# Block means in one bank and three pieces, held stores of x, and a smaller transfer scratch, in an attention and expert kernel on one core

## The chip, the core and the metric

One core of a Trainium2 chip runs one program. Its engines are TensorE (PE), VectorE (DVE), ScalarE (ACT), GpSimd (POOL) and SyncE (SP); they run side by side, each works through its own list in order, and semaphores hold them to one another. PE writes to PSUM banks; DVE and ACT read them. SP and POOL issue the transfers between HBM and SBUF, which share 16 DMA engines. The metric is the device time of one launch in microseconds (us), lower is better.

## The reference

Attention with a local window and block summaries, for 4 batches, 8 heads, 768 positions and 64 channels, then a layer of 8 experts in which each token goes to one expert of bounded size.

```python
k_sum = k.reshape(B, H, nb, block, D).max(axis=3)       # block = 32, nb = 24
v_sum = v.reshape(B, H, nb, block, D).mean(axis=3)
scores_l = scale * q @ k^T, kept where |i - j| < 16
scores_s = scale * q @ k_sum^T + log(block)
a = softmax(concat(scores_l, scores_s))                 # sum + 1e-09
attn = a @ concat(v, v_sum)                             # -> x, 3072 x 512
logits = x @ w_gate                                     # 8 experts
# the largest logits first: each token to one expert, at most 384 tokens each
out[mask_e] = relu(x[mask_e] @ w1[e]) @ w2[e]
```

## The kernel before

**Two parts.** The attention part takes the 24 tiles of 128 query rows in order (t = 0 to 23, six tiles a batch, each tile two units u of 64 rows), writes x to HBM (`xd`) and keeps the logits. The routing picks 384 tokens for each expert in turn; each expert gathers its rows of x, multiplies twice and scatters its result. Only the attention part is touched by the change, with one parameter of the whole program.

**One tile.** PE makes the scores s(t) (four pairs of heads, L365), DVE adds the mask and takes the minimum (m, L373), ACT takes the exponential (e, L380), PE transposes (t, L141), ACT or DVE copies the transposed weights out of PSUM (c, `pt`), PE multiplies them with the window of v (pv, L401), DVE divides by the sum, which is a column of ones beside v (n, L430 to L433, written into `XS[t]`, four buffers in turn), POOL stores the tile (xw, L494), PE transposes x (xt, L141), ACT copies it (xf), and for four tiles at a time PE makes the logits (lg, L472) with a copy, a transpose and a copy behind them (ly, lt, lc).

**One batch.** SP loads keys (`kd`, four loads p = 0 to 3 of 0.41 MB), queries (`qt`) and twelve windows of v (`vw`, 0.2 MB each, task w). From batch 1 on each load waits until an earlier one has landed, so that some 1.3 MB are in flight. DVE takes the maxima of the keys' blocks (`ks`, L289); POOL copies the windows of keys and the maxima into `kw` (two L202 copies for each p; batch 0 has them on ACT and DVE). The block means of v go into the first 24 rows of each of the twelve windows of v: PE multiplies the windows of v with a small matrix (vm, L305, 12 matmuls for each half g of the heads), a copy takes the result out (vmc, `vm`), PE adds the pieces (vb, L332), a copy writes the sums into the first window (vbc, `vw`), and POOL copies them into the other eleven (place, L341).

**PSUM.** Bank x (one buffer) holds the x transposes, and from batch 1 on also each vm and vb. Bank l holds the logits. For batch 0 vm takes x and l, and vb two banks of the output.

**Order.** No order is written down. Every step is a task with an engine (or two to choose from), a cost in us, the tasks that it needs, and a rank; `plan` runs a small model and each time emits the task that can start first, by rank. `TUNE` holds the offsets of the ranks. The order so found is what each engine then follows on the chip, whatever the real times are.

```python
if b:
    @task(("vm", b, g), "pe", 1.6, [("w", u0 + i) for i in range(NQ)] + ["constants"]
          + ([("vbc", b, 0)] if g else [("xf", u0 // 2 - 4)]), u0 - TUNE["vm"] + 0.1 * g)
```

So from batch 1 on, each half of the means needs all twelve windows of v, and the second half also needs the first half's result.

Of the kernel before, what the change touches and what calls it, by code (L numbers as in the profile page):

```python
# [8 lines left out]
F32 = mybir.dt.float32  # L9
# [47 lines left out]
def attention_moe(ctx, tc, qT, kT, v65, wg, w1r, w2r, cst, out, dbg=None, dbi=None):  # L57
# [148 lines left out]
    with ExitStack() as att:  # L206
# [16 lines left out]
        XR = 6  # L223

# [17 lines left out]
        for i in range(2):  # L242
            nc.gpsimd.memset(VW[i][:NB], 0.0)
# [6 lines left out]
        @task("constants2", "sp", 1.4, [], -10, 0.9)  # L250
        def _():
            nc.sync.dma_start(cs[:, CA:], cst[:, CA:CW])
            XS[0] = sb.tile([128, H * D], F32, name="x", bufs=4)
            nc.sync.dma_start(XS[0][:, :TW], cst[:, CW:])
            nc.sync.dma_start(wgs[:, :, :E], wg)
# [16 lines left out]
        for b in range(B):  # L272
# [30 lines left out]
            def means(b, g, k):  # L303
                for j in range(4):
                    nc.tensor.matmul(VP[b, g][32 * j:32 * j + 32], own[:C, k], VW[b % 2][:C, 4 * k + j, 4 * g:4 * g + 4].rearrange("k h d -> k (h d)"), start=k == 0, stop=k == 2)  # L305

            for k in range(3 if b == 0 else 0):
                @task(("vm", 0, k), "pe", 1.0, [("w", 4 * k + i) for i in range(4)] + ["constants"], -TUNE["vm"] + 0.1 * k)
                def _(k=k):
                    for g in range(2):  # L310
                        if k == 0:
                            VP[0, g] = psum.tile([128, 512], F32, name="xl"[g])[:, :4 * VD]
                        means(0, g, k)

            for g in range(2):
                if b:
                    @task(("vm", b, g), "pe", 1.6, [("w", u0 + i) for i in range(NQ)] + ["constants"]
                          + ([("vbc", b, 0)] if g else [("xf", u0 // 2 - 4)]), u0 - TUNE["vm"] + 0.1 * g)
                    def _(b=b, g=g):
                        VP[b, g] = psum.tile([128, 512], F32, name="x")[:, :4 * VD]  # L320
                        for k in range(3):
                            means(b, g, k)

                @task(("vmc", b, g), {"act": 0.42, "dve": 0.4}, None, [("vm", b, g if b else 2)], u0 - TUNE["vm"])
                def _(eng, b=b, g=g):
                    VM[b, g] = sb.tile([128, 4 * VD], F32, name="vm", bufs=2)
                    copy(eng, VM[b, g], VP[b, g])

                @task(("vb", b, g), "pe", 0.45, [("vmc", b, g)], u0 - TUNE["vm"])
                def _(b=b, g=g):  # L330
                    VB[b, g] = psum.tile([128, 512], F32, name="x" if b else f"o{g}")[:NB, :4 * VD]
                    nc.tensor.matmul(VB[b, g], blocks, VM[b, g], start=True, stop=True)  # L332

                @task(("vbc", b, g), {"act": 0.42, "dve": 0.4}, None, [("vb", b, g)] + ([("pv", u0 - 2 * NQ + 1)] if b > 1 else []), u0 - TUNE["vm"])
                def _(eng, b=b, g=g):
                    copy(eng, VW[b % 2][:NB, 0, 4 * g:4 * g + 4].rearrange("k h d -> k (h d)"), VB[b, g])

            for i in range(1, NQ):
                @task(("place", b, i), "pool", 0.58, [("vbc", b, 1)] + ([("pv", (u0 + i - 2 * NQ) | 1)] if b > 1 else []), u0 - TUNE["vm"] + 0.1 * i)
                def _(b=b, i=i):  # L340
                    nc.gpsimd.tensor_copy(VW[b % 2][:NB, i], VW[b % 2][:NB, 0])  # L341
# [4 lines left out]
        for u in range(U):  # L346
# [42 lines left out]
            def _(eng, u=u):  # L389
# [4 lines left out]
                  [("c", u), ("c", u | 1 if t < NT - 1 else u), ("w", u | 1), ("w", u & ~1)] + ([("place", b, (i - s) + x) for x in range(2) if i - s + x] + [("vbc", b, 1)])  # L394
# [14 lines left out]
        def used(t):  # L409
            return ("lg" if t < FOURS else "l", last_of(t))  # L410

        for t in range(NT):
            u = 2 * t + 1
            spare = t >= NT - 2
            for k, half in enumerate(halves(t)):
# [6 lines left out]
                      + ([("xw", t - 4), ("xt", t - 4)] if t >= 4 else []), u + TUNE["n"])  # L422
                def _(t=t, half=half):
                    if half.start == 0:
                        XS[t] = sb.tile([128, H * D], F32, name="x", bufs=4)
# [6 lines left out]
                    for g in gs:  # L432
# [4 lines left out]
                      [("n", t) + me] + [("vbc", b, 1) for b in range(B) if t == max(0, b * NQ // 2 - 3)] + ([("xf", t - 1)] if t and not spare else [("c", U - 1)] if t == NT - 1 else [("xf", t - 1)] if t else []), u + TUNE["xt"])  # L437
# [25 lines left out]
                if t < FOURS:  # L463
                    if t == last_of(t):
                        t0 = t - QUAD + 1

                        @task(("lg", t), "pe", 0.9, [("xf", j) for j in range(t0, t + 1)] + ["constants2"] + ([("lc", t0 - 1)] if t0 else []), u + TUNE["l"])
# [6 lines left out]
                        @task(("ly", t), "act", 0.25, [("lg", t)], u + TUNE["l"] + 0.1)  # L474
                        def _(t=t):
                            LY[t] = sb.tile([128, 128], F32, name="ly")
                            nc.scalar.activation(LY[t], PL[t][:, :128], AF.Copy)
# [14 lines left out]
            @task(("xw", t), "pool", 0.6, [("n", t)], u, 0.73)  # L492
            def _(t=t):
                nc.gpsimd.dma_start(xd[t * 128:(t + 1) * 128], XS[t])  # L494
# [488 lines left out]
```

## Time and profile before

| | us |
|---|---|
| median of 3 runs | 474.02 (473.02 to 474.35) |
| the profiled execution, its own time | 473.94 |
| its span, first to last instruction | 472.2 |
| attention part in the span, to PE's last logits | about 135 |
| PE busy | 444.7 (94%) |
| DVE busy | 337.2 (71%) |
| ACT busy | 226.9 (48%) |
| POOL busy | 126.7 (27%) |

The page gives busy times over the whole span, and a strip of 40 slices of 11.8 us in which the first eight show the DMA engines busy at eight or nine tenths. PE looks busy everywhere, but a matmul counts as busy to its modelled end, so a short wait inside a run of matmuls does not show as idle; how far apart the starts of two rows lie tells more. The chain of work that ended last, followed back from the end, gives the transfers 8% of the span. The trace, asked by stretch, by queue and as a timeline of one engine, gives the rows further below.

### The profile page before, as it was taken

Reading aid. Unit: us, or ns where it says so; the run is one execution under the profiler, and the core shown is the slowest. Engines: PE = TensorE matmul, PEld = TensorE weight load, DVE = VectorE, ACT = ScalarE, POOL = GpSimd, SP = SyncE. Lnnn points to the kernel's source line nnn. Section 1 sums busy time; section 2 is a strip of 40 time slices with the busy share of each in tenths; the row PEclk is TensorE's granted clock in tenths of the full one; section 3 lists DMA queues with packets and bytes.
Section 4 is the critical chain, followed back from the end, with each engine's and each line's share of the span. In section 5 each row is a group of like instructions: output and inputs, shape, how many; then the busy total and the mean of one; then the engine's idle time right before and its main releaser. Section 6 shows DMA issues by size and latency. Waiting matters only on the chain.

```text
span 472.2 us, 12148 instructions
## 1 busy us (share of the span) xinstructions
PE 444.7 (94%) x4598; PEld 369.9 (78%) x4598; DVE 337.2 (71%) x1369; ACT 226.9 (48%) x491; POOL 126.7 (27%) x195
## 2 busy tenths in 40 slices
PE   7999999999974899999999999999999999999992
PEld 6675686877863798788789779878878989989981
DVE  4595888876876987888878977977996962562500
ACT  5676686977810442364354444534444443534410
POOL 9384656516120200230220211202302204102010
PEclk9999999999985899999999999999999999999998
DMA  8989898821210821830851822822741882511001
GB/s 291 267 268 295 273 314 289 252 82 50 84 51 14 300 114 48 292 153 8 291 195 47 275 114 103 286 93 85 237 169 70 278 301 94 190 51 67 1 26 41
DMA packets 25402, 76.23 MB, mean 161 GB/s; under 512 B 3968, under 2 KB 4224, under 8 KB 25344
## 3 DMA queue, kind: packets, MB, share of 16 engines
q1 hardware_dynamic: 19584, 56.58, 35.8%
q0 software_dynamic: 5760, 18.88, 11.6%
q8 instruction: 36, 0.59, 0.5%
q14 instruction: 22, 0.18, 0.1%
HBM read 62.86 MB, written 12.58 MB: 160 GB/s over the span
## 4 chain that ended last, share of the span: by engine, by line
PE 67%; issue 12%; DVE 9%; DMA 8%; POOL 2%; ACT 1%; SPq 0%; POOLq 0%; DVEq 0%; ACTq 0%
PE y L903 24%; PE h L886 18%; PE o L401 4%; PE s L365 4%; DMA kd<-kT 4%; PE t L141 4%; PE x L141 2%; PE h L141 2%; PE x L305 2%; PE r L530 2%; DMA qt<-qT 2%; PE r L553 1%; POOL out L869 1%; DMA vw<-v 1%; DVE g L108 1%
## 5 line engine op out<-in xcount | busy, mean ns | idle before, releaser
L903 PE MATMUL y<-bl,hh 128*128 128x512 f32 x192 | 78.3, 408 | 0.0
L903 PE MATMUL y<-bh,hl 128*128 128x512 f32 x192 | 76.6, 399 | 0.0
L903 PE MATMUL y<-bh,hh 128*128 128x512 f32 x192 | 76.4, 398 | 0.0
L869 POOL DMA_INDIRECT out<-y,idx x24 | 25.4, 1057 | 148.6 <-ACT y L867 127.0
L890 ACT ACTIVATE hh<-h 128x384 fp32r<-128x384 f32 x64 | 31.5, 491 | 66.6 <-PE h L886 64.0
L380 ACT ACTIVATE pe<-sm,mx 128x118 f32<-128x118 f32 x192 | 57.8, 384 | 6.8 <-DVE mx L373 6.7
L886 PE MATMUL h<-xh,ah 128*128 128x384 f32 x256 | 58.6, 342 | 0.6 <-DVE xh L202 0.5
L886 PE MATMUL h<-xh,al 128*128 128x384 f32 x256 | 57.5, 340 | 0.0
L720 POOL DMA_INDIRECT xg<-xd,idx x24 | 24.0, 999 | 123.5 <-issue 90.4
L886 PE MATMUL h<-xl,ah 128*128 128x384 f32 x256 | 56.9, 340 | 0.0
L893 DVE SCALAR_TENSOR_TENSOR hl<-h,hh 128x384 fp32r<-128x384 f32 x64 | 35.0, 550 | 22.0 <-ACT hh L890 21.2
L373 DVE CUSTOM_DVE_ANT_0 sm<-s,cs 128x118 f32<-128x118 f32 x192 | 40.6, 275 | 13.1 <-PE s L365 10.7
L706 ACT ACTIVATE ah<-raw 128x1024 fp32r<-128x1024 f32 (+1 forms) x36 | 33.3, 956 | 33.9 <-DVE best L115 20.6
L886 PEld LDWEIGHTS h<-xh,ah 128*128 128x128 f32 x256 | 45.1, 188 | 2.0 <-DVE xh L202 0.8
L886 PEld LDWEIGHTS h<-xl,ah 128*128 128x128 f32 x256 | 45.2, 188 | 0.4 <-DVE xl L743 0.3
L886 PEld LDWEIGHTS h<-xh,al 128*128 128x128 f32 x256 | 44.9, 188 | 0.0
L903 PEld LDWEIGHTS y<-bh,hh 128*128 128x128 f32 x192 | 36.1, 188 | 6.6
L903 PEld LDWEIGHTS y<-bh,hl 128*128 128x128 f32 x192 | 36.2, 188 | 5.7
L903 PEld LDWEIGHTS y<-bl,hh 128*128 128x128 f32 x192 | 36.2, 188 | 5.6
L709 DVE TENSOR_TENSOR al<-raw,ah 128x1024 fp32r<-128x1024 f32 (+1 forms) x36 | 38.6, 1100 | 0.8 <-ACT ah L706 0.8
L709 DVE TENSOR_TENSOR bl<-raw,bh 128x1024 fp32r<-128x1024 f32 x32 | 38.9, 1215 | 0.0
L740 ACT ACTIVATE xh<-h 128x384 fp32r<-128x384 f32 x28 | 13.7, 493 | 44.7 <-PE h L141 44.7
(169 smaller groups left out, 768.1 us busy)
## 6 DMA issues: line engine op xcount, KB each, us to landing
raw<-w1r SPq DMA_DIRECT2D x32, 512.0 KB
raw<-w2r SPq DMA_DIRECT2D x32, 512.0 KB, 4.5
vw<-v SPq DMA_DIRECT2D x48, 195.0 KB, 4.9
kd<-kT SPq DMA_DIRECT2D x16, 399.0 KB, 6.2
qt<-qT SPq DMA_DIRECT2D x12, 512.0 KB, 5.8
xd<-x POOLq DMA_DIRECT2D x24, 256.0 KB
xg<-xd,idx POOLq DMA_INDIRECT x24
out<-y,idx POOLq DMA_INDIRECT x24
```

Source lines behind the costliest of these rows:

```text
L141: nc.tensor.transpose(o, i, idn)
L365: nc.tensor.matmul(PS[2 * t + k][x * 64:x * 64 + 64, p], QT[b % 2][r, (i + x) // FIRST, p, (i + x) % FIRST], kw[b, p][r, i + x], start=Tru ...
L373: nc.vector.tensor_tensor_reduce(sm[:, p], PS[u][:, p], m, -0.125, 3e38, op0=OP.add, op1=OP.min, accum_out=mx[:, p:p + 1])
L380: nc.scalar.activation(PE_[u][:, p], SM[u][0][:, p], AF.Exp, bias=SM[u][1][:, p:p + 1], scale=-1.0)
L706: nc.scalar.activation(hi[:, c], raw[:, c], AF.Copy)
L709: nc.vector.tensor_tensor(lo[:, c], raw[:, c], hi[:, c].bitcast(F32), op=OP.subtract)
L720: nc.gpsimd.indirect_dma_start(out=x, out_offset=None, in_=xd, in_offset=bass.IndirectOffsetOnAxis(ap=idx[:, c:c + 1], axis=0))
L869: st = nc.gpsimd.indirect_dma_start(out=out, out_offset=bass.IndirectOffsetOnAxis(ap=ROUND[r][1][:, c:c + 1], axis=0), in_=y, in_offset=None)
L886: nc.tensor.matmul(ph, a[:, d], b[:, d], start=n == 0, stop=n == 11)
L890: nc.scalar.activation(hh[:, f], ph, AF.Relu)
L893: nc.vector.scalar_tensor_tensor(hl[:, f], ph, 0.0, hh[:, f].bitcast(F32), op0=OP.max, op1=OP.subtract)
L903: nc.tensor.matmul(py[c], a[:, f, s], b, start=f == 0 and i == 0, stop=f == 7 and i == 2)
```

## The change

Three things change. (1) The means of both halves g share one bank, `l`, as `[128, 2, 4, 64]`: the column of ones is left out (the memset of `VW` writes ones once), and vm is three tasks, one for each four windows of v, for every batch. vb's two matmuls go into one bank, `l` (batch 0: `x`), from batch 1 on both after both copies. The four-tile logits, which use bank `l` too, now wait for the means. (2) The first eight tiles of x have buffers of their own (`xk`), their stores wait for the last copy of batch 3's means, and the division waits for an earlier store only from tile 12 on. (3) The scratch of the transfers that POOL issues is set to 4096 bytes a partition. The copy `ly` moves into a buffer of transposed x, whose next writer now waits for lt.

```diff
+        HELD = 8
+
+        def rows(t):
+            return sb.tile([128, H * D], F32, name="xk", bufs=HELD) if t < HELD else sb.tile([128, H * D], F32, name="x", bufs=4)
...
-            nc.gpsimd.memset(VW[i][:NB], 0.0)
+            nc.gpsimd.memset(VW[i][:NB], 1.0)
...
             def means(b, g, k):
                 for j in range(4):
-                    nc.tensor.matmul(VP[b, g][32 * j:32 * j + 32], own[:C, k], VW[b % 2][:C, 4 * k + j, 4 * g:4 * g + 4].rearrange("k h d -> k (h d)"), start=k == 0, stop=k == 2)
-
-            for k in range(3 if b == 0 else 0):
-                @task(("vm", 0, k), "pe", 1.0, [("w", 4 * k + i) for i in range(4)] + ["constants"], -TUNE["vm"] + 0.1 * k)
...
+                    nc.tensor.matmul(VP[b][32 * j:32 * j + 32, g], own[:C, k], VW[b % 2][:C, 4 * k + j, 4 * g:4 * g + 4, :D], start=k == g == 0, stop=k == 2, skip_group_check=True)
+
+            for k in range(3):
+                @task(("vm", b, k), "pe", 1.0, [("w", u0 + 4 * k + i) for i in range(4)] + ["constants"] + ([("vm", b, k - 1)] if k else [("vbc", 0, g) for g in range(2)] if b == 1 else [("lc", 4 * b - 1)] if b else []), u0 - TUNE["vm"] + 0.1 * k)
+                def _(b=b, k=k):
+                    if k == 0:
+                        VP[b] = psum.tile([128, 2, 4, D], F32, name="l")
...
-                if b:
-                    @task(("vm", b, g), "pe", 1.6, [("w", u0 + i) for i in range(NQ)] + ["constants"]
-                          + ([("vbc", b, 0)] if g else [("xf", u0 // 2 - 4)]), u0 - TUNE["vm"] + 0.1 * g)
...
-                @task(("vb", b, g), "pe", 0.45, [("vmc", b, g)], u0 - TUNE["vm"])
...
+                @task(("vb", b, g), "pe", 0.45, [("vmc", b, j) for j in range(2) if b or j == g] + ([("vb", b, 0)] if g else []), u0 - TUNE["vm"])
                 def _(b=b, g=g):
...
+                        VB[b] = psum.tile([128, 2, 4, D], F32, name="l" if b else "x")[:NB]
+                    nc.tensor.matmul(VB[b][:, g], blocks, VM[b][:, g], start=True, stop=True)
...
         def used(t):
-            return ("lg" if t < FOURS else "l", last_of(t))
+            return ("lt" if t < FOURS else "l", last_of(t))
...
-                      + ([("xw", t - 4), ("xt", t - 4)] if t >= 4 else []), u + TUNE["n"])
+                      + ([("xw", t - 4), ("xt", t - 4)] if t >= HELD + 4 else []), u + TUNE["n"])
...
-                        XS[t] = sb.tile([128, H * D], F32, name="x", bufs=4)
+                        XS[t] = rows(t)
...
+                        @task(("lg", t), "pe", 0.9, [("xf", j) for j in range(t0, t + 1)] + ["constants2"] + ([("lc", t0 - 1)] if t0 else []) + [("vbc", {3: 1, 11: 2, 15: 3}[t], g) for g in range(2) if t in (3, 11, 15)], u + TUNE["l"])
...
-                            LY[t] = sb.tile([128, 128], F32, name="ly")
+                            LY[t] = XTS[t0][:, 0]
...
-            @task(("xw", t), "pool", 0.6, [("n", t)], u, 0.73)
+            @task(("xw", t), "pool", 0.6, [("n", t)] + ([("place", B - 1, NQ - 1)] if t < HELD else []), u, 0.73)
...
-    nc = _bacc.Bacc("TRN2", target_bir_lowering=False, num_devices=1)
+    nc = _bacc.Bacc("TRN2", target_bir_lowering=False, num_devices=1, dynamic_dma_scratch_size=4096)
```

Since `plan` finds the order anew, every engine's list in the attention part differs a little; the lists of the routing and the experts are the same. Three places follow, before and then now, with the lines of each kernel.

PE at the block means of batch 1 (`vw_102` is batch 1's v, `vw_101` batch 0's, `o` the outputs, s with `qt_100` the scores of batch 1). Before, after tile 5's first half of the output:

```order
L141 MATMUL t<-cs,pe 118x128 x8
L401 MATMUL o_861<-vw_101,pt 64x65 x8
L305 MATMUL x<-vw_102,cs 32x260 x12
L365 MATMUL s_901<-kw,qt_100 64x118
L365 MATMUL s_902<-kw,qt_100 64x118
```

Now, after tile 3's first half, where the third piece follows one tile later:

```order
L141 MATMUL x<-cs,xk 128x128 x4
L141 MATMUL t<-cs,pe 118x128 x4
L400 MATMUL o_715<-vw_101,pt 64x65 x8
L309 MATMUL l<-vw_102,cs 32x256 x8
L400 MATMUL o_716<-vw_101,pt 64x65 x8
L141 MATMUL t<-cs,pe 118x128 x4
L309 MATMUL l<-vw_102,cs 32x256 x8
L364 MATMUL s_795<-kw,qt_100 64x118
L364 MATMUL s_796<-kw,qt_100 64x118
```

The means moved ahead by nearly two tiles and lie between other work in pieces of eight.

DVE at the first maximum of batch 2, `ks<-kd`. Before it came behind the mask work of tile 6 and the divisions up to tile 4:

```order
L373 ISA sm,mx<-s_777,cs 128x118
L373 ISA mx 128x1
L289 TENSOR_REDUCE ks<-kd 128x24
L373 ISA sm,mx<-s_901,cs 128x118
L373 ISA mx 128x1
```

Now both copies of batch 1's means stand ahead of it, and the division of tile 4 (`xk<-o`) behind it:

```order
L202 COPY vm<-l 128x256 x2
L293 TENSOR_REDUCE ks<-kd 128x24
L202 COPY pt<-t 118x512
L429 TENSOR_SCALAR dn<-o_815 128x4
L429 TENSOR_SCALAR dn<-o_816 128x4
L430 RECIPROCAL dn<-dn 128x8
L432 TENSOR_TENSOR xk<-o_815,dn 128x256
L432 TENSOR_TENSOR xk<-o_816,dn 128x256
L293 TENSOR_REDUCE ks<-kd 128x24
L372 ISA sm,mx<-s_908,cs 128x118
```

A copy of transposed weights, a division and a second maximum moved between the first maximum and the mask work of tile 7; the list's mask work of tile 6 stays ahead.

POOL in the second half of the attention part (`kw<-kd` and `kw<-ks` are the two copies for each p, `vw<-vw` x11 the copies of the means). Before, from the window copies of batch 3 to the last store:

```order
L494 DMA xd<-x 128x512
L202 COPY kw<-kd 128x12x94 x2
L202 COPY kw<-ks 128x12x24 x2
L202 COPY kw<-kd 128x12x94
L202 COPY kw<-ks 128x12x24
L494 DMA xd<-x 128x512
L202 COPY kw<-ks 128x12x24
L341 COPY vw_101<-vw_101 24x520 x11
L494 DMA xd<-x 128x512 x7
L341 COPY vw_102<-vw_102 24x520 x11
L494 DMA xd<-x 128x512 x6
```

Now the same stretch begins with the last window copies; the eight held stores are the ones of `xk`:

```order
L202 COPY kw<-kd 128x12x94
L493 DMA xd<-x 128x512
L202 COPY kw<-ks 128x12x24
L340 COPY vw_101<-vw_101 24x520 x11
L493 DMA xd<-x 128x512 x3
L202 COPY kw<-ks 128x12x24
L493 DMA xd<-x 128x512
L202 COPY kw<-ks 128x12x24
L493 DMA xd<-x 128x512
L340 COPY vw_102<-vw_102 24x520 x11
L493 DMA xd<-xk 128x512 x8
L493 DMA xd<-x 128x512 x8
```

The first eight stores moved behind batch 3's copies, ahead of the stores of tiles 16 to 23; and the copy of batch 2's last maxima, ks(2,3), which before stood ahead of all window copies of batch 3, now stands behind the first two of them, with the store of tile 8 between those.

## Rows read from the trace of the kernel before

**Rows 1.** Busy us (x instructions) of PE, PEld, DVE, ACT, POOL; PEclk, DMA share, GB/s.

```profile
51.20:96.00 44.80, 44.80 (x887) 34.39 (x891) 39.40 (x223) 35.67 (x105) 27.78 (x46) 1.00 0.90 284
96.00:134.90 38.90, 38.90 (x774) 30.76 (x762) 28.64 (x184) 29.54 (x85) 11.49 (x21) 1.00 0.18 64
```

**Rows 2.** SP's queue (q1), 22 to 31.7 us: packets, MB, share of 16 engines.

```profile
q1 hardware_dynamic: 929, 2.65, 86.4%
```

**Rows 3.** Queues of SP (q1) and POOL (q0), 31.7 to 48.4 us.

```profile
q1 hardware_dynamic: 1557, 3.45, 67.9%
q0 software_dynamic: 400, 1.31, 19.9%
```

**Rows 4.** Chain of waits, 25 to 60 us: start, us, what.

```profile
43.11 5.27 DMA kd<-kT
```

**Rows 5.** DVE timeline: start, us, line, operation, [idle before <-releaser].

```profile
48.47 0.95 DVE L289 TENSOR_REDUCE ks<-kd 128x24 f32<-128x768 f32 x1 [5.80 <-DMA kd<-kT]
49.34 0.27 DVE L373 CUSTOM_DVE_ANT_0 sm<-s,cs 128x118 f32<-128x118 f32 x1
...
50.94 0.41 DVE L202 COPY vw<-x 24x260 f32<-24x260 f32 x1
51.27 0.67 DVE L202 COPY pt<-t 118x512 f32<-118x512 f32 x1
51.87 0.21 DVE L430 TENSOR_SCALAR dn<-o 128x4 f32<-128x4 f32 x2
...
53.02 0.94 DVE L289 TENSOR_REDUCE ks<-kd 128x24 f32<-128x768 f32 x1
```

**Rows 6.** PE timeline (each fp32 matmul has two records).

```profile
42.09 2.82 PE L305 MATMUL x<-vw,cs 118*32 118x260 f32 x20
45.34 0.63 PE L305 MATMUL x<-vw,cs 118*32 118x260 f32 x2 [0.43 <-DMA vw<-v]
...
51.16 0.63 PE L365 MATMUL s<-kw,qt 64*64 64x118 f32 x14 [0.42 <-DVE mx L373]
...
63.09 1.04 PE L365 MATMUL s<-kw,qt 64*64 64x118 f32 x32
64.06 0.66 PE L141 MATMUL x<-cs,x 128*128 128x128 f32 x4
64.64 1.15 PE L401 MATMUL o<-vw,pt 118*64 118x65 f32 x32
...
78.05 1.52 PE L305 MATMUL x<-vw,cs 118*32 118x260 f32 x24
79.50 0.64 PE L365 MATMUL s<-kw,qt 64*64 64x118 f32 x16
80.07 0.69 PE L401 MATMUL o<-vw,pt 118*64 118x65 f32 x16
80.69 0.62 PE L332 MATMUL x<-vm,cs 128*24 128x260 f32 x2
81.23 0.69 PE L401 MATMUL o<-vw,pt 118*64 118x65 f32 x16
```

**Rows 7.** Queues, 31.7 to 71.9 us.

```profile
q1 hardware_dynamic: 4004, 9.24, 74.1%
q0 software_dynamic: 719, 2.36, 15.1%
```

**Rows 8.** POOL timeline.

```profile
71.98 1.14 POOL L202 COPY kw<-kd 128x1128 f32<-128x1128 f32 x1 [4.08 <-DMA kd<-kT]
...
100.07 0.54 POOL L494 DMA_DIRECT2D xd<-x  x1 [3.66 <-DVE x L433]
...
110.66 6.26 POOL L341 COPY vw<-vw 24x520 f32<-24x520 f32 x11
```

**Rows 9.** Stores of x: ns min/median/max, first and last start.

```profile
L494 POOL DMA_DIRECT2D xd<-x x24: 542/542/739, 31.7 to 134.2; - x24
```

**Rows 10.** One store alone, the columns of rows 1.

```profile
101.00:102.00 1.00, 1.00 (x25) 0.81 (x28) 1.00 (x11) 1.00 (x4) 0.00 (x0) 1.00 0.69 262
```

More of the change, by code (lines that the diff above doesn't have):

```diff
@@ L252, in _ @@
             nc.sync.dma_start(cs[:, CA:], cst[:, CA:CW])
-            XS[0] = sb.tile([128, H * D], F32, name="x", bufs=4)
+            XS[0] = rows(0)
             nc.sync.dma_start(XS[0][:, :TW], cst[:, CW:])
@@ L313, in _ @@
-                        means(0, g, k)
+                        means(b, g, k)
             for g in range(2):
-                if b:
-                    @task(("vm", b, g), "pe", 1.6, [("w", u0 + i) for i in range(NQ)] + ["constants"]
-                          + ([("vbc", b, 0)] if g else [("xf", u0 // 2 - 4)]), u0 - TUNE["vm"] + 0.1 * g)
[L319 to L322, printed above, removed]
@@ L324, in _ @@
[L324 to L329 removed]
+                @task(("vmc", b, g), {"act": 0.42, "dve": 0.4}, None, [("vm", b, 2)], u0 - TUNE["vm"])
+                def _(eng, b=b, g=g):
+                    if b not in VM:
+                        VM[b] = sb.tile([128, 2, 4, D], F32, name="vm")
+                    copy(eng, VM[b][:, g], VP[b][:, g])
@@ L330, in _ @@
+            for g in range(2):
+                @task(("vb", b, g), "pe", 0.45, [("vmc", b, j) for j in range(2) if b or j == g] + ([("vb", b, 0)] if g else []), u0 - TUNE["vm"])
                 def _(b=b, g=g):
-                    VB[b, g] = psum.tile([128, 512], F32, name="x" if b else f"o{g}")[:NB, :4 * VD]
-                    nc.tensor.matmul(VB[b, g], blocks, VM[b, g], start=True, stop=True)
+                    if g == 0:
+                        VB[b] = psum.tile([128, 2, 4, D], F32, name="l" if b else "x")[:NB]
+                    nc.tensor.matmul(VB[b][:, g], blocks, VM[b][:, g], start=True, stop=True)
@@ L393, in _ @@
             @task(("pv", u), "pe", TUNE["cp"],
-                  [("c", u), ("c", u | 1 if t < NT - 1 else u), ("w", u | 1), ("w", u & ~1)] + ([("place", b, (i - s) + x) for x in range(2) if i - s + x] + [("vbc", b, 1)])
+                  [("c", u), ("c", u | 1 if t < NT - 1 else u), ("w", u | 1), ("w", u & ~1)] + ([("place", b, (i - s) + x) for x in range(2) if i - s + x] + [("vbc", b, 0), ("vbc", b, 1)])
                   + ([("n", t - 1)] if t else []) + ([("pv", u - 1)] if s else []), u)
@@ L436, in _ @@
                 @task(("xt", t) + me, "pe", TUNE["cx"] * part / H,
-                      [("n", t) + me] + [("vbc", b, 1) for b in range(B) if t == max(0, b * NQ // 2 - 3)] + ([("xf", t - 1)] if t and not spare else [("c", U - 1)] if t == NT - 1 else [("xf", t - 1)] if t else []), u + TUNE["xt"])
+                      [("n", t) + me] + ([("xf", t - 1)] if t and not spare else [("c", U - 1)] if t == NT - 1 else [("xf", t - 1)] if t else []), u + TUNE["xt"])
                 def _(t=t, d0=d0, d1=d1):
```

10 lines of the change are left out of this document (3 added, 7 removed).

## The prediction

> **What bounds the kernel now.** I read the table of stretches first, then the transfer queues of the stretches that stood out, then the chain of waits, then the timelines of DVE, PE and POOL there. From 51.2 us to the end of the attention part at 134.9 us PE is never idle, 44.80 of 44.80 and 38.90 of 38.90 us, while DVE stays under 90% [rows 1]; there only less PE work helps. Before 51 us it is otherwise. The chain runs through transfers alone, last the load of the first keys of batch 2 (kd(2,0), 5.27 us, landed at 48.38) [rows 4]. DVE shows why this matters: it stood for 5.80 us until 48.47 in front of the maximum over kd(2,0), with the mask work of tile 7 queued behind it [rows 5]. PE shows the other half: its first 20 records of batch 1's block means took 2.82 us where 24 need 1.45, then it waited for another load of v, and the scores of tile 8 could only go on at 51.16 [rows 6]. What the loads share the engines with is in the queues: from 31.7 to 48.4 us, SP's loads moved 3.45 MB and POOL's stores of x 1.31 MB, five stores, which took 19.9% of the engines' time [rows 3]. From 22 to 31.7 us there is no store yet, and the same loads, with the same limit on what is in flight, moved 2.65 MB in 9.7 us, 273 GB/s against 207 [rows 2].
>
> **Held stores.** The first eight tiles keep buffers of their own and are stored after the last copy of batch 3's means, so five stores leave the stretch before 48.4 and three more the one after it. Bound by the engines' time given back, the loads end 0.199 x 16.7 = 3.3 us sooner; by bytes at the rate without stores, 3.45 MB / 273 GB/s = 12.6 us in place of 16.7, 4.1 us sooner. I take 4.1, since the rate was seen under the same limit, and kd(2,0) lands at 44.3.
>
> What is late next is DVE. In the new order the two copies of the means (VMC) stand ahead of the maximum over kd(2,0), and behind it one copy of transposed weights, the division of tile 4, the second maximum and the mask work of tile 7. From the rows these are 0.87, 0.60, 1.15, 0.95 and 1.60 us [rows 5], 5.2 in all, so tile 8's scores start at 49.6, 1.5 us sooner than 51.16. By then PE has more behind it than before: the second half of the means (1.45 us), both block sums in one visit (0.5) and one x transpose (0.58) [rows 6], 2.5 us that before came later. Together 4.0 us. Going down PE's own list instead, with the v loads of the three pieces landing at about 37.7, 39.8 and 42.9 by the same rate, it reaches tile 8 at 50.1, worth 3.5. I take **-4.0**, with 3.3 (the share) and 4.5 (all five stores at the stretch's whole rate) as ends.
>
> **Means in one bank, in three pieces.** The matmuls are as many (24 a batch) with 256 columns for 260, below 0.1 us in all. Each piece needs only its own four v loads, which is what lets PE take them up while the last eight are in flight; that is in the 4.0 above. What else changes is how often PE changes its tiling. Counting in the two orders, it changes 98 times after the start of tile 8 before and 82 times now. A score block in one run takes 0.97 us (63.09 to 64.06), and half a block 0.57 (79.50 to 80.07) [rows 6], so one cut costs 0.17 and each of its two changes 0.08. 16 x 0.08 = **-1.3**; nothing covers them, since PE is full there. The ends are 0.8 and 1.6. Batch 1's copies move to DVE ahead of the maximum (already in the list above); over the whole part DVE gets five copies more, some 2.5 us, beside a PE that runs on. Memset to one, the logits' copy in a buffer of transposed x and the waits of the four-tile logits on the shared bank have a slack of over a microsecond on PE's list: nothing, and about 0.5 us for each batch if it is gone.
>
> **POOL's new order** is where I add something. The copy ks(2,3), which the fourth quarter of tile 12's scores needs, now stands behind the window copies of kd(3,0) and kd(3,1). Before, the first of these waited for its load until 71.98 [rows 8]. From 31.7 to 71.9 the loads moved 9.24 MB; at 273 GB/s that is 33.8 us, landing at 65.5; by the share of the stores (15.1% of 40.2) at 65.8 [rows 7]. kd(3,1), 0.41 MB, follows 1.5 us later, the window copy takes 1.1, the small one 0.4: ks(2,3) at 68.6 to 68.9. PE's list, 4.5 us ahead by then, asks for it at 68.35. I take **+0.5**.
>
> **The burst at the end.** The eight held stores stand between batch 3's copies and the store of tile 16, whose buffer the division of tile 20 writes. From the second means matmul: about 1.3 us to the copies, 11 copies at 6.26 us, nine issues at 0.54 (median of all 24 stores, 0.739 the longest) and 1.9 us from an issue at 100.07 to its last byte before 102.00, 14.4 us in all [rows 8 to 10]. PE's list from there to the end of tile 20 sums to 18. Three microseconds of slack: nothing. The routing's gathers of x are over 20 us away.
>
> **The smaller scratch** has no row. The bounds are nothing and, if POOL has to wait for room, an issue that lasts until its data has moved, 1.9 us for 0.54; the case is below. I take nothing, as no stretch has more than nine POOL transfers at once.
>
> **Sum.** The profiled execution took 473.94 us, its span 472.2, and the median of three runs is 474.02, so they stand for each other. 473.94 - 4.0 - 1.3 + 0.5 = 469.1. The routing and the experts after 134.9 keep their order and move as a block.
>
> **The rivals.**
> - *POOL takes part of it back* (0.19). The loads win only the 3.3 us of the first five stores, because SP also waits for buffers that free no sooner. Then kd(3,0) lands at 68.6, ks(2,3) is there at 71.7, and tile 12 waits 3.3 us in place of 0.5: 471.9. For it: a coupling that the old order did not have. Against: SP's waits for other things than loads are short, and PE frees the buffers sooner too.
> - *The loads do not speed up* (0.10). Each load waits for an earlier one to land, so if that round trip does not shorten, kd(2,0) still lands at 48.4; DVE's longer list then puts tile 8 at 53.6, 2.5 us later, against 2.5 us of work done ahead, and only the tiling changes are left: 472.7, within the 0.3% that a measurement of this kernel can tell from no change. Against it stands [rows 2].
> - *More* (0.07): 4.5 and 1.6 with no wait at tile 12, 467.8.
> - *The burst blocks the attention's last tiles* (0.07), the slower side. If each held store takes until its data has moved, nine take 17.1 us for 4.9, and the store of tile 16 lands 12.2 us later; past the slack of 3, the division of tile 20 waits 9, and PE's next output with it: 469.1 + 9 = 478. It decides from an issue of 0.54 + 3 / 9 = 0.9 us on. For it: the smaller scratch, with eight transfers queued at once. Against: the 24 stores were issued in 0.542 to 0.739 us [rows 9], most of them beside a busy DVE. The Trainium skill ("SBUF — State Buffer", SBUF: two separate sides, the box on DVE blocking DMA) has a rule that speaks for this case: descriptors that POOL writes stall while DVE holds the port that both share, 0.62 us alone becoming 3.1. By that price nine issues would take 28 us and the kernel about 488. The trace does not agree so far: no store took over 0.74 us.
>
> **How the numbers follow.** The forecast's own case has 0.57: the relief passes to PE, between 467.8 and 470.5. With the rivals the sum is one. Faster by over 0.3% (below 472.6) are the forecast, the first and the third, 0.83; within 0.3%, 0.10; slower, 0.07. The range from 467.4 to 472.2 holds the forecast, "more" and POOL's case, 0.83.
>
> **What would show it.** No store of x on the queue before about 100 us, and loads near 270 GB/s from 31.7 on. The maximum over kd(2,0) at about 44.3, its wait on DVE down from 5.80 to about 1 us. Batch 1's means in three pieces at about 37 to 43 with waits under 1.5 us each. Tile 8's scores at 49.6 to 50.1. Attention's last PE work at about 130 us. Wrong would be: loads that still run at 207 GB/s, a PE wait of over 1 us at tile 12, held stores issued in more than 0.9 us, or a division of tile 20 that waits for a store.

## The result, and the profile after

The changed kernel takes 470.45 us (median of 17 runs, 466.08 to 473.58) where the kernel before takes 473.43 (17 runs, 471.89 to 476.23). The ratio (time after over time before, by fast runs alone) is 0.9911, with a 95% interval from 0.9888 to 0.9934: by it the changed kernel is 4.2 us faster, between 3.1 and 5.3. The medians lie 3.0 us apart, so a difference between two kernels is known to about a microsecond, and the text says each time whether it goes by ratios or by medians. The prediction said 469.1, from 467.4 to 472.2. The time is right; the path to it is right only in part, as the rest of this section and the experiments show.

First the stretches of the kernel after, in the columns of [rows 1].

```profile
31.70:44.00 12.30, 10.58 (x179) 6.52 (x178) 7.02 (x38) 6.02 (x17) 5.62 (x8) 1.00 0.79 225
51.20:96.00 44.80, 43.43 (x909) 35.24 (x909) 38.93 (x234) 36.49 (x109) 23.79 (x40) 1.00 0.85 257
```

PE, full from 51.2 us on before, now loses 1.37 us between 51.2 and 96. From 31.7 to 44 the DMA engines are busy for 0.79 of the time only, although PE stands still for 1.7 us there. The loads alone, from 22 to 31.7 us and from 31.7 to 48.4 (they answer to [rows 2, 3]; POOL's queue has no line in either, so the held stores are indeed gone from here):

```profile
q1 hardware_dynamic: 781, 2.29, 77.1%
...
q1 hardware_dynamic: 1809, 3.97, 81.5%
```

3.97 MB in 16.7 us are 238 GB/s, 15% more than the 207 of [rows 3] but not the 273 on which the first term was built. What holds them back is in the chain of waits from 25 us on and in the rate by slices from 31.7 to 48.4 us (40 slices of 0.42 us; the first line is the busy share in tenths):

```profile
29.95 7.33 DMA qt<-qT
37.30 0.31 SPq L230
...
40.61 4.67 DMA vw<-v
...
DMA  9898796999742204767699998999899899798898
GB/s 367 222 290 324 285 277 199 219 269 274 155 100 85 69 25 65 159 244 120 224 324 354 249 194 214 324 344 289 228 268 252 306 322 314 306 229 237 336 321 252
```

SP may not issue the next loads of v before a load of queries, 7.33 us under way, has landed, and in the eleventh to seventeenth slice, 35.9 to 38.8 us, the rate falls to between 25 and 159 GB/s and the busy share from seven tenths to under one: the engines have little to do. PE shows what came of it (this and the next two are timelines, as [rows 6], [rows 5] and [rows 8]):

```profile
37.50 1.52 PE L309 MATMUL l<-vw,cs 118*32 118x256 f32 x12 [0.64 <-DMA vw<-v]
...
41.42 1.54 PE L309 MATMUL l<-vw,cs 118*32 118x256 f32 x12 [0.64 <-DMA vw<-v]
...
45.33 1.05 PE L309 MATMUL l<-vw,cs 118*32 118x256 f32 x10 [0.23 <-DMA vw<-v]
46.31 0.66 PE L141 MATMUL x<-cs,xk 128*128 128x128 f32 x4
...
53.31 1.04 PE L364 MATMUL s<-kw,qt 64*64 64x118 f32 x32
...
72.72 0.43 PE L364 MATMUL s<-kw,qt 64*64 64x118 f32 x8 [1.37 <-POOL kw L202]
...
133.76 0.68 PE L406 MATMUL s<-wgs,xr 128*64 128x8 f32 x16
...
134.71 0.67 PE L529 MATMUL r<-oh,g 128*128 128x8 bf16 x21 [0.27 <-DVE L L498]
```

```profile
46.42 0.76 DVE L202 COPY vm<-l 128x256 f32<-128x256 f32 x2 [0.64 <-PE l L309]
47.09 0.94 DVE L293 TENSOR_REDUCE ks<-kd 128x24 f32<-128x768 f32 x1
```

Each of the three pieces of batch 1's means waits for v, the last until 45.33. The copies of the means on DVE follow the last piece, and the maximum over kd(2,0) follows them at 47.09. It no longer waits for its load (the 5.80 us of [rows 5] are gone), but it begins only 1.4 us earlier than 48.47, and tile 8's scores, with more work put ahead of them, start at 53.31. PE does not wait for DVE there as it did before (0.42 us in [rows 6]): from the end of the last piece, at 46.31, it goes down its own list without a wait and reaches tile 8 7.00 us later. It takes the same 7.00 us in all six profiles with the new means and held stores. So what sets tile 8 is the last load of v for the means, which landed at 45.28, with PE's list behind it, and not DVE. POOL's timeline shows tile 12 and the burst:

```profile
69.35 1.13 POOL L202 COPY kw<-kd 128x1128 f32<-128x1128 f32 x1 [10.49 <-DMA kd<-kT]
...
71.16 1.14 POOL L202 COPY kw<-kd 128x1128 f32<-128x1128 f32 x1
72.22 0.44 POOL L202 COPY kw<-ks 128x288 f32<-128x288 f32 x1
...
111.22 4.26 POOL L493 DMA_DIRECT2D xd<-xk  x8
```

ks(2,3), the last of these copies, stands behind two window copies of batch 3, the first of which waited for its load until 69.35, and PE's fourth quarter of tile 12 starts at 72.72, as soon as this copy has ended. The eight held stores go out in 4.26 us, 0.53 each, and no engine of the attention part waits for them.

**Where the time went.** The attention part's last PE work starts at 133.76 where it was 134.96: 1.2 us. The timeline of before has

```profile
134.96 0.68 PE L407 MATMUL s<-wgs,xr 128*64 128x8 f32 x16
135.91 0.67 PE L530 MATMUL r<-oh,g 128*128 128x8 bf16 x21 [0.27 <-DVE L L499]
```

and the second line is the first matmul of the routing, at 134.71 in the profile after. From there to the issue of the last scatter the profile after is 0.9 us longer (329.41 for 328.52). Yet its span is 3.8 us shorter. The rest is at the very end. These are the heads of the two answers and the last scatter on POOL, before and after:

```profile
core 0 of [0], span 472.2 us
...
464.43 0.96 POOL L869 DMA_INDIRECT out<-y,idx  x1 [4.63 <-DVE y L865]
...
core 0 of [0], span 468.4 us
...
464.12 0.96 POOL L868 DMA_INDIRECT out<-y,idx  x1 [4.16 <-DVE y L864]
```

From the issue of the last scatter to the end of the span 7.8 us pass before and 4.3 after. No busy instruction lies there in either. In both the scatter's own last bytes move within 2.4 us of the issue; behind them there is no data transfer either, for some 5.5 us before and 2 us after. So in this pair of profiles 3.5 of the 3.8 us come from behind the last scatter, which the prediction did not look at, and where no work of the attention part lies.

### The profile page after: what moved, and what is told of

It is laid out like the page before. It is cut to its first block, busy times and chain, and to the rows that moved or that the text cites. A ratio compares the mean times of both kernels' runs of the same rounds, so it can differ in the third digit from the quotient of the medians.

```text
span 468.4 us, 12140 instructions
## 1 busy us (share of the span) xinstructions
PE 441.3 (94%) x4598; PEld 368.8 (79%) x4598; DVE 339.2 (72%) x1374; ACT 224.4 (48%) x486; POOL 126.5 (27%) x195
## 4 chain that ended last, share of the span: by engine, by line
PE 64%; issue 12%; DVE 9%; DMA 9%; POOL 2%; SPq 1%; ACT 0%; POOLq 0%; DVEq 0%; ACTq 0%
PE y L902 22%; PE h L885 18%; PE t L141 4%; PE o L400 4%; PE s L364 3%; DMA vw<-v 3%; DMA qt<-qT 3%; PE x L141 2%; PE l L309 2%; PE h L141 2%; DMA kd<-kT 2%; PE r L529 2%; POOL out L868 1%; PE r L552 1%; DVE g L108 1%
## 5 line engine op out<-in xcount | busy, mean ns | idle before, releaser
L705 ACT ACTIVATE ah<-raw 128x1024 fp32r<-128x1024 f32 (+1 forms) x36 | 33.4, 957 | 31.8 <-DMA raw<-w1r 31.7
```

The lines of the kernel that those rows point to most:

```text
L705: nc.scalar.activation(hi[:, c], raw[:, c], AF.Copy)
```

## The experiments

Three theories stood against each other: that the loads' relief and the tiling changes carry the gain (the prediction's), that the smaller scratch carries it, and, for what the held stores bring, that the loads are limited by what may be in flight and not by the engines that the stores took. The first four kernels do one part of the change or two without the third. The changed kernel with the large scratch was not tried: the eight held buffers leave no room for it.

**The scratch alone.** The kernel before, with

```diff
-    nc = _bacc.Bacc("TRN2", target_bir_lowering=False, num_devices=1)
+    nc = _bacc.Bacc("TRN2", target_bir_lowering=False, num_devices=1, dynamic_dma_scratch_size=4096)
```

> The kernel before with the scratch for dynamic transfers at 4096 bytes and nothing else. The theory of the prediction: nothing, ratio 1.000 (473.4 us), attention's last PE work at 135 us and about 7.8 us from the issue of the last scatter to the end of the span, as before. The theory of the end, formed from the two traces: before spends 7.8 us after its last scatter is issued and after only 4.3, and the smaller scratch does this; then this kernel takes 469.9 us, ratio 0.9926, with the attention part as before and 4.3 us behind the last scatter.

471.23 us, ratio 0.9944 (0.9925 to 0.9964). Its last scatter, as above:

```profile
core 0 of [0], span 467.0 us
...
462.90 0.96 POOL L869 DMA_INDIRECT out<-y,idx  x1 [4.15 <-DVE y L865]
```

4.1 us to the end. The smaller scratch is worth 2.7 us by the ratio, 3.1 by the medians and 3.7 at the end of the trace, and "nothing" was wrong.

**The means alone.** The kernel after, without held stores and with the large scratch:

```diff
-        HELD = 8
+        HELD = 0
-    nc = _bacc.Bacc("TRN2", target_bir_lowering=False, num_devices=1, dynamic_dma_scratch_size=4096)
+    nc = _bacc.Bacc("TRN2", target_bir_lowering=False, num_devices=1)
```

> The means in one bank and in three pieces, with no store held and the large scratch. The theory of the prediction: fewer tiling changes, 1.3 us, and little of the loads' term, so 472.1 us, ratio 0.997, with attention's last PE work at about 134 us and 7.8 us behind the last scatter. The theory of the end: the large scratch keeps the long end, and what the attention part wins (1.2 us at 134 us) is down to 0.3 us by 191 us, so 473.1 us, ratio 0.999.

472.40 us, ratio 0.9941 (0.9906 to 0.9976), a scattered kernel (468.94 to 477.22). Its end is long again, 7.9 us, which ties the end to the scratch and not to the attention part:

```profile
core 0 of [0], span 468.8 us
...
460.94 0.96 POOL L868 DMA_INDIRECT out<-y,idx  x1 [4.63 <-DVE y L864]
```

The scratch theory's 473.1 was too high: the means bring 2.8 us by the ratio (1.9 by the medians), and the prediction's 0.997 lies in the interval.

**Means and scratch.** The kernel after with `HELD = 0` and nothing else.

> The means in one bank with the smaller scratch, no store held. The theory of the prediction: as with the large scratch, 472.1 us, ratio 0.997, and 3.5 us slower than the changed kernel less the held stores' share. The theory of the end: 469.6 us, ratio 0.992, with 4.3 us behind the last scatter, the same as the changed kernel within 0.5 us.

467.70 us, ratio 0.9857 (0.9812 to 0.9902): 3.5 us below the scratch alone by the medians, 4.1 by the ratios, and the intervals of the two do not meet. Both theories expected it slower. The means in one bank are worth more than either gave them, and no run shows the kernel slower without the held stores than with them. Its profile fell on the slowest of its six runs (471.03), in which PE waits 3.41 us for v at 99.66, so it does not stand for the kernel.

**Held stores and scratch.** The kernel before with the stores held, the means as they were:

```diff
+        HELD = 8
+        def rows(t):
+            return sb.tile([128, H * D], F32, name="xk", bufs=HELD) if t < HELD else sb.tile([128, H * D], F32, name="x", bufs=4)
...
-                      + ([("xw", t - 4), ("xt", t - 4)] if t >= 4 else []), u + TUNE["n"])
+                      + ([("xw", t - 4), ("xt", t - 4)] if t >= HELD + 4 else []), u + TUNE["n"])
...
-            @task(("xw", t), "pool", 0.6, [("n", t)], u, 0.73)
+            @task(("xw", t), "pool", 0.6, [("n", t)] + ([("place", B - 1, NQ - 1)] if t < HELD else []), u, 0.73)
```

with the smaller scratch.

> The kernel before with the first eight stores held and the smaller scratch (which makes the room), the means as before. The theory of the prediction: loads near 270 GB/s from 31.7 us on, DVE's wait for the first keys of batch 2 down from 5.8 us to under 3, and 3.3 us less, 470.1 us, ratio 0.993, with the gain seen at attention's last PE work (about 131.5 us). The theory of the end: attention's last PE work at 134 to 135 us, 4.3 us behind the last scatter, 469.9 us, ratio 0.9926. The times are close; the place of the gain tells them apart.

468.96 us, ratio 0.9885 (0.9855 to 0.9916): 2.3 us below the scratch alone by the medians, 2.8 by the ratios. So holding the stores helps where the means stand as before. But not by loads at 270 GB/s; SP's queue and the slices from 31.7 to 48.4 us:

```profile
q1 hardware_dynamic: 1692, 3.73, 76.1%
...
GB/s 183 241 378 353 187 104 249 219 144 284 344 145 64 20 25 15 135 284 120 184 329 364 279 304 279 318 284 289 254 226 321 311 255 329 260 115 130 130 260 329
```

223 GB/s, with the same hole around 37 us, here down to 15. Of the 1.31 MB that the stores moved here before, the loads took up about 0.25 (3.73 for 3.45 to 3.50). DVE still waits 4.32 us for the first keys of batch 2, and the attention part's last PE work starts at 133.88: the place in which the prediction would see the gain (131.5) does not show it. The traces can't say where the 2.3 us lie, since this profile is of the slowest of six runs and the one of the scratch alone of the fastest of twelve. Alone, the two attention edits bring 2.8 and 4.1 us over the small scratch by the ratios; together, in the changed kernel, only 1.6 (0.9911 against 0.9944). They do not add.

**A smaller scratch still, with and without held stores.** The changed kernel, and the same with `HELD = 0`, both with

```diff
-    nc = _bacc.Bacc("TRN2", target_bir_lowering=False, num_devices=1, dynamic_dma_scratch_size=4096)
+    nc = _bacc.Bacc("TRN2", target_bir_lowering=False, num_devices=1, dynamic_dma_scratch_size=1024)
```

> The changed kernel with a scratch of 1024 bytes in place of 4096. Theory of the end, from four traces: behind the issue of the last scatter 7.8 us pass with 16384 bytes (two traces, 7.77 and 7.86) and 4.1 to 4.3 with 4096 (four traces), 0.30 us for each KB; so 3.3 us here, 0.9 less than the changed kernel, ratio to before about 0.989. Rival, the prediction's burst case brought about by a scratch that is really too small: POOL waits for room, a held store takes over 0.9 us to issue in place of 0.54, and the kernel is slower than the changed one.

> The means in one bank, no store held, scratch of 1024 bytes: the run beside it without the held stores. Prediction's theory (held stores free the engines for the loads): about 3.5 us slower than the run with held stores at the same scratch, ratio about 0.997. Theory formed since: from 31.7 to 48.4 us the loads moved 3.45 to 3.82 MB beside stores and 3.73 to 3.97 without, so holding them gives them at most a tenth, and ks(2,3) behind the next windows makes tile 12 wait; then this run is as fast or up to 2 us faster, ratio 0.984 to 0.989, with 3.3 us behind the last scatter.

469.79 us, ratio 0.9926 (0.9890 to 0.9961), and 468.35, ratio 0.9888 (0.9842 to 0.9934). The last scatter of the first, and its held stores:

```profile
core 0 of [0], span 467.4 us
...
463.19 0.97 POOL L868 DMA_INDIRECT out<-y,idx  x1 [4.64 <-DVE y L864]
...
L493 POOL DMA_DIRECT2D xd<-xk x8: 539/539/548, 109.4 to 113.1; - x8
```

4.2 us to the end in both, as with 4096: the theory of 0.30 us for each KB falls. POOL does not wait for room even with this scratch (0.548 us at most for a held store), so the burst case falls too. For the held stores beside the new means this is the second pair, and both point the same way: with them the kernel is 1.8 us slower here by the ratios, and 2.6 in the pair at 4096. The intervals overlap in each, so a loss is likely and not settled; a gain of 3.5 us from the held stores, as the expectations took it from the first term, is excluded.

**More loads in flight.** The changed kernel, with the limit that the loads on the chip obey raised, the planner's left alone, so that every engine's order stays:

```diff
-    def behind(sizes, size):
+    def behind(sizes, size, limit=TUNE["ahead"]):
...
-        while k >= 0 and ahead + sizes[k] <= TUNE["ahead"]:
+        while k >= 0 and ahead + sizes[k] <= limit:
...
-                tc.add_manual_dep(st.ins, LOADS[behind([z for _, z in LOADS], size)][0].ins.name, ...
+                tc.add_manual_dep(st.ins, LOADS[max(0, behind([z for _, z in LOADS], size, 2.0))][0].ins.name, ...
```

> The changed kernel with up to 2.0 MB of loads in flight in place of 1.3 (the order on every engine is the same; only which earlier load each load waits for changes). Theory: without stores the loads are held back by that limit and not by the engines, so with it lifted they move 31.7 to 48.4 at over 260 GB/s in place of 238, the pieces of batch 1's means wait less (1.5 us in all before) and the time falls by 1 to 2 us against the changed kernel, ratio about 0.988. Rival: the rate stays at 220 to 240 GB/s since something else bounds it, and the time stays within 0.5 us of the changed kernel, ratio 0.991.

467.91 us, ratio 0.9872 (0.9829 to 0.9915), 1.8 us less than the changed kernel by the ratios, with intervals that overlap. The trace is clearer. SP's queue from 22 to 31.7 us, then queue and slices from 31.7 to 48.4 us, the DVE timeline and the PE timeline:

```profile
q1 hardware_dynamic: 1075, 3.12, 97.1%
...
q1 hardware_dynamic: 2006, 4.61, 102.2%
...
GB/s 273 278 288 179 219 204 259 239 264 294 254 279 264 323 254 269 262 296 257 210 251 196 244 329 352 413 382 391 336 352 385 279 169 166 318 265 295 196 334 334
...
44.17 0.94 DVE L293 TENSOR_REDUCE ks<-kd 128x24 f32<-128x768 f32 x1
...
36.53 1.08 PE L309 MATMUL l<-vw,cs 118*32 118x256 f32 x16
38.74 1.31 PE L309 MATMUL l<-vw,cs 118*32 118x256 f32 x16
41.56 1.90 PE L309 MATMUL l<-vw,cs 118*32 118x256 f32 x16
43.39 0.66 PE L141 MATMUL x<-cs,xk 128*128 128x128 f32 x4
...
50.39 1.04 PE L364 MATMUL s<-kw,qt 64*64 64x118 f32 x32
...
130.08 0.68 PE L406 MATMUL s<-wgs,xr 128*64 128x8 f32 x16
```

276 GB/s, no slice below 166, no piece of the means waits, the maximum over kd(2,0) starts at 44.17, tile 8 at 50.39 and the last PE work of attention at 130.08. That is the prediction's own picture (273, 44.3, 49.6 to 50.1, 130), row by row. It needed a limit of 2.0 MB, which the change does not have. The limit also binds from 22 to 31.7 us, the stretch that the prediction took its rate from: raised, the loads move 3.12 MB there, and 2.99 and 3.05 in the two later kernels with this limit, where with 1.3 MB in flight it is 2.27 to 2.68 in all eleven profiles. The wait at tile 12 is gone as well, since kd(3,0) comes earlier.

**POOL's order.** The changed kernel with ks(2,3) put ahead of batch 3's windows (the planner then also regroups a few score blocks of PE):

```diff
-                @task(("win", b, p), ..., [("k", b, p)] + free, u0 - TUNE["mx"] + p)
+                @task(("win", b, p), ..., [("k", b, p)] + free + ([("ks", 2, HP - 1)] if b == 3 else []), u0 - TUNE["mx"] + p)
```

> The changed kernel with POOL's copy ks(2,3) put ahead of the window copies of batch 3 again. Theory: PE's wait at tile 12 (1.37 us, 0.5 in the prediction) goes, attention ends about 1.2 us earlier and so does the kernel, ratio about 0.989. Rival: the later windows put off what comes next on POOL, another wait of 1 us or more takes its place by 96 us, and the time stays, ratio 0.991.

467.23 us, ratio 0.9852 (0.9817 to 0.9888), 2.6 us by the medians below the changed kernel at 1024 bytes on the same chip (0.9926, 0.9890 to 0.9961; the intervals just part). Against the changed kernel at 4096 bytes (0.9888 to 0.9934) they touch. PE is full again from 51.2 to 96 us:

```profile
51.20:96.00 44.80, 44.80 (x930) 35.97 (x927) 41.23 (x240) 37.36 (x114) 22.64 (x38) 1.00 0.81 253
```

So the wait at tile 12 is one place where the two edits together lose what each brings alone. In none of the five profiles with one of the two attention edits alone does PE wait for this copy: in the order without held stores ks(2,3) stands ahead of batch 3's windows anyway (65.67 and 73.24 in the means alone). The wait is 1.4 us in the trace; by the first matmul of the routing the two profiles differ by 1.5 us (131.31 against 132.84). The other 1.1 us of the medians are not placed, nor is the rest of what fails to add.

**Both repairs, and the limit without held stores.** First the last two edits together, then the raised limit in the kernel with `HELD = 0`.

> Both repairs of the changed kernel at once: ks(2,3) ahead of batch 3's windows, and up to 2.0 MB of loads in flight. If the two waits they take away are different ones, their gains add: 2.6 and 1.9 us against the changed kernel at the small scratch, so about 465.7 us where before takes 474.5, ratio 0.981. Rival: both relieve the same stretch of PE before 75 us, and it is no better than the better of the two, ratio 0.985.

> Means in one bank, scratch 4096, up to 2.0 MB of loads in flight, no store held. If the loads are held back by the limit alone and stores cost them little, this is as good as the changed kernel with the same limit: ratio 0.987 or below, with loads of 4.3 MB or more from 31.7 to 48.4 us. If the stores take the engines' time once the limit is lifted, the loads stay below 4.0 MB there (4.61 with the stores held) and the ratio stays at that of the means alone, 0.986 to 0.989.

467.07 us, ratio 0.9844 (0.9815 to 0.9873), and 467.26, ratio 0.9861 (0.9830 to 0.9892). The repairs do not add, as the rival said: both take away the wait at tile 12. And the loads of the second kernel, SP's queue and POOL's from 31.7 to 48.4 us:

```profile
q1 hardware_dynamic: 1890, 4.23, 83.1%
q0 software_dynamic: 368, 1.22, 19.7%
```

4.23 MB next to 1.22 MB of stores, as much as the changed kernel moves with no store beside its loads (3.97 to 4.43 in three profiles). Lifting the limit does for the loads what holding the stores does. With it lifted the stores still take something (4.55 and 4.61 without them), yet the time shows no difference.

**A middle scratch, and the changed kernel again.** The kernel before with a scratch of 8192 bytes, and the changed kernel as it is.

> The kernel before with a scratch of 8192 bytes. Behind the issue of the last scatter 7.8 us pass with 16384 bytes and 4.2 with 4096 and with 1024, so the end is not proportional. Theory A, a floor of 4.2 us under something that grows with the scratch: between 4.2 and 6.0 us here, ratio 0.994 to 0.998. Theory B, a step that comes only with the full size: 4.2 us, ratio 0.994, as with 4096.

> The changed kernel once more, as it is, beside the repairs on the same chip: ratio 0.991 as in the first comparison, 4.2 us behind the last scatter. Its profile shows how far one execution's loads stand for the kernel: 3.97 MB from 31.7 to 48.4 us in the first one, 4.43 with the scratch of 1024 bytes, in the same order. Where the wait at tile 12 (1.37 and 1.39 us in those two) is there for the third time, it belongs to the order and not to the execution.

470.81 us, ratio 0.9919 (0.9895 to 0.9944), with the last scatter here:

```profile
core 0 of [0], span 470.0 us
...
465.52 0.96 POOL L869 DMA_INDIRECT out<-y,idx  x1 [4.63 <-DVE y L865]
```

4.5 us to the end. With 16384 bytes it was 7.8 and 7.9, with 8192 it is 4.5, with 4096 and 1024 between 4.1 and 4.3 in every profile shown here. Halving the scratch once brings nearly all; below 8192 there is a floor of 4.2 us. The end that theory A gave (4.2 to 6.0) holds, the ratio of 0.994 lies at the edge of the interval, and 0.998 is excluded. That the scratch sets the end is shown. What happens there is not: behind the scatter's last byte no row of the trace lies in it. The Trainium skill ("Runtime: NRT & Kernel Launch", The ~15µs preamble/postamble breakdown) lists, behind each kernel, a barrier with a reset of the DMA rings, together about 2 us, with no size in it. Whether the 3.6 us are that reset no run here shows.

The changed kernel took 468.70 us, ratio 0.9906 (0.9867 to 0.9944), the same as the first time. In this profile the loads move 4.17 MB, and tile 12 waits less:

```profile
71.05 0.43 PE L364 MATMUL s<-kw,qt 64*64 64x118 f32 x8 [0.77 <-POOL kw L202]
```

So the wait is there in all three profiles of this order (1.37, 1.39, 0.77 us) and belongs to it.

The milestones side by side, from one profile each: MB that SP's queue moved from 31.7 to 48.4 us, start of tile 8's scores, first matmul of the routing, issue of the last scatter, and what then passes to the end of the span.

| kernel | MB | tile 8 | routing | scatter | to the end |
|---|---|---|---|---|---|
| before | 3.45 | 51.16 | 135.91 | 464.43 | 7.8 |
| before, scratch 4096 | 3.50 | 48.80 | 133.54 | 462.90 | 4.1 |
| before, scratch 8192 | 3.48 | 50.59 | 136.15 | 465.52 | 4.5 |
| after | 3.97 | 53.31 | 134.71 | 464.12 | 4.3 |
| after, again | 4.17 | 52.25 | 133.04 | 462.70 | 4.2 |
| after, scratch 1024 | 4.43 | 51.42 | 132.84 | 463.19 | 4.2 |
| after, ks(2,3) first | 4.37 | 51.35 | 131.31 | 459.98 | 4.2 |
| after, 2.0 MB in flight | 4.61 | 50.39 | 131.03 | 459.56 | 4.2 |
| after, both | 4.55 | 51.06 | 131.81 | 461.27 | 4.2 |

One profile does not stand for a kernel to better than about 1.5 us either way: the first three have the same order up to the routing and reach it between 133.54 and 136.15. The others reach it at 134.83 (held stores alone), 132.56 (means alone), 135.96 (means and scratch, its slowest run), 134.01 (means, scratch 1024) and 130.83 (means and scratch, 2.0 MB in flight).

## Why the prediction was right in its time and only half right in its reasons

The sum was -4.0 - 1.3 + 0.5 = -4.8, all of it in the attention part, and nothing for the scratch. By the means of the three profiles of the old order and the three of the new, the routing starts at 135.2 and 133.5: the attention part brings 1.7 us, a third of the sum. The end brings 3.5. Two errors of some 3 us, of opposite sign, left the forecast within 1.4 us of the median. That is luck. Of its own signs of being wrong one came: a wait of over 1 us at tile 12.

- **Held stores, -4.0: the step that failed is the rate.** "By bytes at the rate without stores, 3.45 MB / 273 GB/s" took the rate of one execution from 22 to 31.7 us (2.65 MB) for what the loads do without stores. Under the limit of 1.3 MB that stretch gives 2.27 to 2.68 MB, so 2.65 is near the top. In the next stretch the loads move 238, 250 and 265 GB/s in the three profiles of this order, held up in each by a load of queries that is 6.0 to 7.3 us under way. The bound by share took the engines' time for what is scarce; the stores had in part used time that the loads did not fill, as the held stores alone showed. The path behind it was wrong too. "What is late next is DVE" does not hold: PE waits for no DVE ahead of tile 8 in any profile of the new order. The path is the one that the prediction worked out beside it, PE's own list from the last load of v. The pieces were to have their loads by 42.9 and got the last at 45.28, and tile 8 starts at 53.31, 52.25 and 51.42 in place of 49.6 or 50.1. In the one profile where the loads do run at 276 GB/s the step's numbers come out to within 0.8 us, so the relief was right in kind, and the rate was what kept it small. The rival that had the reason, "each load waits for an earlier one to land", got 0.10; it put tile 8 at 53.6, and the truth lies between it and the forecast.
- **Work ahead of tile 8: right. Fewer tiling changes, -1.3: too small.** From tile 8's scores to the first matmul of the routing PE takes, less its waits above 0.3 us, 84.7 or 84.8 us in the three profiles of the old order and 80.0 in all three of the new. That is 4.7 us shorter; the prediction had 2.5 moved ahead and 1.3 for the tiling, 3.8. The groups of instructions in this stretch tell which was low. The work moved ahead is the one that the prediction priced at 2.5: 24 records of the means, two of a block sum and four of an x transpose are gone from here. The outputs, the transposes of weights and the scores keep theirs, and yet take less (count | busy us, mean ns | idle, before and after):

```profile
L401 PE MATMUL o<-vw,pt 118*64 118x65 f32 x576 | 22.0, 226 | 0.0
L141 PE MATMUL t<-cs,pe 128*118 128x128 f32 x136 | 21.0, 281 | 0.0
L365 PE MATMUL s<-kw,qt 64*64 64x118 f32 x510 | 17.8, 269 | 0.4 <-DVE mx L373 0.4
...
L400 PE MATMUL o<-vw,pt 118*64 118x65 f32 x576 | 21.0, 225 | 0.0
L141 PE MATMUL t<-cs,pe 128*118 128x128 f32 x137 | 20.5, 279 | 0.0
L364 PE MATMUL s<-kw,qt 64*64 64x118 f32 x512 | 17.1, 268 | 1.4 <-POOL kw L202 1.4
```

  That is 2.2 us for 16 changes fewer, 0.14 each for the 0.08 that the prediction read from one cut score block. No kernel tried the order of these groups by itself, so that the tiling is all of it is argued.
- **POOL's new order, +0.5: right place, low by the same rate.** kd(3,0) lands at 69.35 and not at 65.5, and tile 12 waits 1.37 us in place of 0.5. The rival that priced this at 3.3 was too high.
- **The burst at the end: right.** Eight stores in 4.26 us, no wait on DVE, issues of 0.539 to 0.548 us with a quarter of the new scratch. The Trainium skill's price ("SBUF — State Buffer", SBUF: two separate sides) of 3.1 us for a transfer that POOL issues beside a copy on DVE which holds the shared port shows in none of these issues. DVE's copies beside them last 0.3 us at most, so these stores hardly test that price.
- **The smaller scratch, nothing: wrong.** It was looked for only where POOL issues. The bounds named nothing and a loss, and left out a gain, although the trace of before had 7.8 us between its last scatter and its end in which no engine works and, after the first 2.4, no transfer either.
- **Moving as a block: right to about a microsecond either way.** From the first matmul of the routing to the last scatter the profiles in the table take 328.5 to 330.4 us, with the same order in all; the 0.9 us given back in the first pair is within that.

**What is at least as fast.** The new means with the smaller scratch and no held store takes 467.70 us, ratio 0.9857 (0.9812 to 0.9902); the changed kernel with ks(2,3) moved ahead 467.23; with the limit raised too 467.07, ratio 0.9844 (0.9815 to 0.9873). These cannot be told from one another, and only the last is clear of the changed kernel's interval in the first comparison (0.9888 to 0.9934). The first is the simplest: it leaves out the held stores, and no run shows that they are missed.

## What to carry to other kernels

Before you move a transfer out of another's way, ask what limits the other: if loads wait for earlier loads, holes in the rate by slices show it, and freeing the engines gives back only part of the share. A rate read from one execution is one draw; look at a second before you build a term on it. Two edits may not add, and together they can bring an order, and so a wait, that neither has alone; run each alone. A resource that a program reserves also has a price outside its use, so look at the first and the last microseconds of the span too, and where a term has no row, let its bounds reach below nothing.

## What the runs showed of the hardware

The end of the program, from the issue of the last indirect scatter, took 7.8 and 7.9 us with a scratch for dynamic transfers of 16384 bytes, 4.5 with 8192, and 4.1 to 4.3 with 4096 or 1024; the scatter's bytes take the first 2.4 us of it. Issues cost the same with each, 0.54 us for a store of 0.26 MB. With at most 1.3 MB in flight and no store beside them, the loads move between 2.27 and 2.68 MB from 22 to 31.7 us, from one execution to the next (2.27, 2.59 and 2.67 in three profiles of one order); with 2.0 MB in flight they move 2.99 to 3.12.
